# Four places in an attention and mixture-of-experts kernel where an instruction moves in its engine's order

## The chip, the cores and the metric

The kernel runs on one core of a Trainium2 chip. The metric is the device time of one launch in microseconds, less is better. The engines are named as in the profile: PE (TensorE, matrix products), PEld (its weight loads), DVE (VectorE), ACT (ScalarE), POOL (GpSimd), SP (SyncE, which issues most DMA transfers).

## What is computed

Causal attention with a bias from running sums, then a two-level mixture of experts over its output. All data are float32.

```python
cum = np.cumsum(np.maximum(s, 0.0), axis=-1)
bias = -(cum[:, :, :, None] - cum[:, :, None, :])
scores = np.where(causal, -1000000000.0, q @ k.T / 8 + np.minimum(bias, 0.0))
attn = softmax(scores)            # 8 batches, 8 heads, 576 tokens, 64 wide
x = (attn @ v) as rows of 512     # 4608 tokens
# each token: best of 4 groups, then best of its 4 experts; weight = both softmax values
out[tok] = weight * (relu(x[tok] @ w1[g, e]) @ w2[g, e])   # 512 -> 1024 -> 512
```

## The kernel before

**Attention.** The 64 heads go in 32 pairs, and the main loop takes one head a step. A step's instructions stand in an order written out by hand: strings of letters (`ORDERS`, `FIRST`, `OPENING`), one letter for one piece of work, so that PE, DVE, ACT and POOL each get theirs interleaved. For the step's own head there are the scores (B, five products into PSUM, then `exp` on ACT with b and the causal mask on POOL with e), for the head before it the product with v (C, evacuated on ACT with v), and for a head four steps on the row maximum of the scores (A0 to A5: products `pm`, which DVE reduces with a, tile `mx`, into `mc`). The six pieces of the row maximum are, in the order of their numbers, 288 keys (the first half of the last query tile), 64, 192, 320, 448, and 288 again (its second half). `pm` has two PSUM banks, so a product `pm` waits until DVE has reduced the one two before it.

When a pair is done its output is divided by the sums of the softmax. DVE transposes the sums in blocks (Y, L333), inverts one column (Z, L339), transposes back (W, `back`, L344) and multiplies (K, `finish`, L354, which writes `xT`). W stands in the even steps; K comes at the start of the odd step that follows, since that step asks for it (`need`).

**Running sums.** At the start DVE rounds s up to 0 and scales it (`r1`), makes running sums of 64 heads by 576 tokens in one instruction (`c2`, L440), splits them in a high and a low part (`cumh`, named `ch` in the profile, L441 and L442), and SP copies rows of them into the operand tiles `WA` of the first four pairs (`load_a`, L177). `ones(i)` sets the rows of ones in `WA[i]`: for 0 and 2 on DVE, for 1 and 3 on POOL. The first products of all (L208) need the high and low rows.

**Router.** Every four pairs one batch of 576 tokens is routed (`Router.batch`, called a piece at a time with R): logits, a transposition of the last 64 tokens into rows (`pr`, L754, copied to `xrt` on ACT, L756), choice of group and expert, places in the experts' lists (`rows`, `val`, and products `pi` for token numbers, `pw` for weights, L863). PSUM tiles of the scores, of the logits and of `pr` share a ring of three banks (`ring`, pool `ps_s`); the router also has one bank of its own (`kept`, pool `ps_t`).

**Experts.** The first expert begins while the last batch is still being routed. Its PE order is fixed by `behind` (the first named instruction comes after the second): `pi` of the last batch stands after 8 of the products `py` of its second layer (`made[8]` comes after it). From `pi` DVE makes the row numbers by which POOL gathers the tokens. What the first expert has beyond 256 tokens is done as a small extra tile (`Tile`, name "r"), whose scaled output `yo` goes into a tile of `rows(u)`: one buffer that the 256 tokens' output `yr` has just used. Output rows leave by indirect DMA from POOL (`scatter`, L967). The other 15 experts follow, with weights loaded a megabyte at a time (`raw`, L1001) and split in two parts on ACT, POOL and DVE.

Outside the order by hand (DVE, ACT and POOL from the last two steps of the attention to the second expert) a scheduler sets the order.

Of the kernel before, what the change touches and what calls it, by code (L numbers as in the profile page):

```python
# [8 lines left out]
F32 = mybir.dt.float32  # L9
# [4 lines left out]
ALU = mybir.AluOpType  # L14
# [5 lines left out]
B, H, S, D = 8, 8, 576, 64  # L20
P = 128
NTOK = B * S
DM = 512
# [14 lines left out]

KT = [(P * k, min(P, S - P * k), S - P * k) for k in range(5)]
Q2 = 256  # L40
W2 = S - Q2


# [68 lines left out]
def attention(tc, qk, v, s, wr, xs, st):  # L112
# [3 lines left out]
    with ExitStack() as ctx:  # L116
# [36 lines left out]
        def split(p, h, later=False):  # L153

            r, w, wb = raws[p], WA[p % NA], WB[p % NBB]
            nc.scalar.copy(w[0:64, :, h, QO:], r[:, h])

            def low(a):
                i = nc.gpsimd.tensor_tensor(  # L159
                    out=wb[64 * a:64 * a + 64, a, h], in0=r[:, h, a], in1=w[0:64, a, h, QO:].bitcast(F32),  # L160
                    op=ALU.subtract)
                if gate and gate[0] is not None:
                    tc.add_manual_dep(i.ins, gate[0].ins.name, mybir.DependencyInfo(
                        mybir.DependencyClass.Sync, mybir.DependencyReason.DATA), reason="behind the product")

            for a in (KA, QA):
                if later:
                    push("G", p, lambda a=a: low(a))
                else:
                    low(a)  # L170

        def load_a(p):
            w = WA[p % NA]
            if p < 4:
                for h in range(2):
                    n = 2 * p + h
                    nc.sync.dma_start(w[64:66, KA, h, QO:].bitcast(F32), cumh[n:n + 1].bitcast(F32))  # L177
            else:
                nc.sync.dma_start(w[64:66, KA, :, QO:].bitcast(F32), cumd[2 * p:2 * p + 2].rearrange("h a s -> a h s"))

# [251 lines left out]

        def ones(i):
            for a in (QA, KA):
                (nc.gpsimd if i % 2 else nc.vector).memset(WA[i][64:66 if a == QA else 68, a].bitcast(F32).rearrange("p h q -> p (h q)"), 1.0)

        ones(0)
        nc.vector.tensor_scalar(out=r1, in0=s0, scalar1=0.0, scalar2=8.0, op0=ALU.max, op1=ALU.mult)

        nc.vector.tensor_tensor_scan(out=c2, data0=r1, data1=r1, initial=0.0, op0=ALU.add, op1=ALU.max)  # L440
        nc.vector.tensor_copy(cumh[:, 0], c2)  # L441
        nc.vector.tensor_tensor(out=cumh[:, 1], in0=c2, in1=cumh[:, 0].bitcast(F32), op=ALU.subtract)  # L442
        ones(2)
        ones(1)

        mask = sm.tile([P, S], F32, name="mask", tag="mask", bufs=1)
# [12 lines left out]
        load_a(1)  # L459
        for h in range(2):  # L460
            split(0, h)
        load_b(0)
        for t in VT:
            nc.gpsimd.memset(t[:, 0:NB, 2], 1.0)
# [9 lines left out]
        def store_sums():  # L474
# [8 lines left out]

        ORDERS = [o.split() for i, o in enumerate((
# [4 lines left out]
        FIRST = [o.split() for i, o in enumerate((  # L489
# [122 lines left out]
class Router:  # L612
# [121 lines left out]
    def batch(self, b, x):  # L734
# [14 lines left out]
        self.logits(b, x)  # L749
        yield  # L750

        ps = self.ps_s(f"pr{b}")
        for c in range(4):
            nc.tensor.transpose(ps[:64, c * P:(c + 1) * P], x[:, c, 512:S], ident)  # L754
        xr = sm.tile([64, DM], F32, name=f"xrt{b}", tag="xrt", bufs=1)
# [181 lines left out]
def moe(tc, w1, w2, xs, st, out):  # L937
# [3 lines left out]
    with ExitStack() as ctx:  # L941
# [87 lines left out]
        def rows(u):  # L1029
            return sp.tile([P, 3, DM], F32, name=f"yr{u}", tag="yr", bufs=1)  # L1030
# [217 lines left out]
        class Tile:  # L1248
# [8 lines left out]
            def items(self):  # L1257
                u, w = self.u, self.w

                th, tl = xhl(u, 1)  # L1260
                h = self.xg[:, 0:2].rearrange("p a c -> p (a c)")
                pss = {}

                def split(hi, lo, src, j, cols):
                    ps = pt.tile([P, 512], F32, name=f"pr{u}_{j}", tag="pt")
                    for c in range(4):
                        nc.tensor.transpose(ps[:, c * P:(c + 1) * P], src[:, c * P:(c + 1) * P], ident)
                    pv = ps.rearrange("p (a c) -> p a c", c=cols)
                    return (nc.scalar.copy(hi, pv),
                            V.tensor_tensor(out=lo, in0=pv, in1=hi.bitcast(F32), op=ALU.subtract))  # L1270

                def x():
                    self.split = split(th[:, :, 0:P], tl[:, :, 0:P], self.xg[:, 2], "x", P)

                def hidden(i, c0):
                    if c0 == 0:
                        pss[i] = acc(f"pu{u}_{i}")
                    for c in range(c0, c0 + 2):
                        for n, (a, b) in enumerate(((th, w.h), (tl, w.h), (th, w.l))):
                            nc.tensor.matmul(pss[i], a[:, c, 0:P], b[i][:, c], start=(c == 0 and n == 0),  # L1280
                                             stop=(c == 3 and n == 2))
                    if c0 == 2:
                        nc.scalar.activation(h[:, i * 512:(i + 1) * 512], pss[i], AF.Relu)

                def turn(j):
                    cs = slice(2 * j, 2 * j + 2)
                    split(th[:, cs, P:], tl[:, cs, P:], h[:, j * 512:(j + 1) * 512], j, 256)

                def y(f0):
                    if f0 == 0:  # L1290
                        pss["y"] = acc(f"pv{u}")
                    for f in range(f0, f0 + 2):
                        fs = slice(P + P * (f % 2), 2 * P + P * (f % 2))
                        for n, (a, b) in enumerate(((th, w.h), (tl, w.h), (th, w.l))):
                            nc.tensor.matmul(pss["y"], a[:, f // 2, fs], b[2 + f // 4][:, f % 4],
                                             start=(f == 0 and n == 0), stop=(f == 7 and n == 2))
                    if f0 == 6:
                        yo = rows(u)[:, 0]
                        V.tensor_scalar(out=yo, in0=pss["y"], scalar1=self.cw, scalar2=None, op0=ALU.mult)
                        scatter(yo, self.ids)  # L1300

                return ([x] + [lambda i=i, c=c: hidden(i, c) for i in range(2) for c in (0, 2)] +
                        [lambda j=j: turn(j) for j in range(2)] + [lambda f=f: y(f) for f in (0, 2, 4, 6)])
# [69 lines left out]
        with tc.manual_schedule(engines={ENG.PE}):  # L1373
            run(X)
            behind(tc, first.turns[0], st.av[0])
            behind(tc, st.av[2], first.turns[3])
            for i in st.put_off:
                behind(tc, i, first.split[1])
            for i in range(4):
                behind(tc, wts[0].casts[i], first.highs[1 if i < 2 else 3])  # L1380
            behind(tc, first.highs[2], st.evacs[-1])
            behind(tc, wts[0].lows[14], rest.last)
            h = first.h_items()
            run(h)
            made = first.products
            behind(tc, made[34], st.logged)
            behind(tc, st.turning, made[54])
            behind(tc, made[55], st.turned)
            behind(tc, made[77], st.counted)
            behind(tc, st.powers, wts[0].casts[11])  # L1390
            for i in [st.thirds] + first.rounds[4:]:
                behind(tc, i, wts[0].casts[15])
            Y, R = first.y_items(), rest.items()
            del made[:]
            run(Y[:5])
            behind(tc, made[8], st.listed[0])
            behind(tc, st.listed[2], made[-4])
            run(Y[5:6])
            run(R[:1])
            with after(tc, rest.split[1]):  # L1400
                by_slot(idp, idlp, 0, E)
                listed = V.tensor_copy(ids, idp)
            part = [st.lists[:, j].rearrange("p e h -> p h e") for j in range(NV)]
            cwl = idl
            with after(tc, listed):
                V.tensor_copy(idlp, part[3])
                V.tensor_tensor(out=idlp, in0=idlp, in1=part[4], op=ALU.add)
                V.tensor_tensor(out=cwl, in0=idlp, in1=part[2], op=ALU.add)
                V.tensor_copy(idlp, cwl)
                by_slot(cws, idlp, 0, 1)  # L1410
            run(Y[6:] + R[1:5])
            W = wts[1].load((first.rounded, rest.split[0], None, None), (None, rest.split[1], None, None))
            run(W[:8])
            low = wts[1].low
            X, Z = slots[1].x_items(), first.z_items()
            run(X[:2] + R[5:6] + X[2:])
            with after(tc, *slots[1].split):
                run(W[8:12])
            run(R[6:7] + Z)
            with after(tc, *slots[1].split):  # L1420
                run(W[12:])
            run(R[7:])
            with after(tc, low):
                slots[2].gather()
# [244 lines left out]
```

## Time and profile before

| | |
|---|---|
| median of 3 runs | 899.67 us (899.33 to 900.61) |
| the profiled execution | 901.16 us, its span 899.4 us |
| busy in the span: PE, DVE, ACT, POOL | 95%, 77%, 68%, 69% |
| attention alone, about 30 to 420 us | PE busy 98 to 99% of each stretch |
| first expert's end, 440 to 460 us | PE busy 17.41 of 20 us, granted clock 0.91 |
| second expert's start, 480 to 500 us | PE busy 18.42 of 20 us |

PE is the engine that is nearly always busy; the others have room. Matmuls are pipelined and their modelled ends overlap, so a short wait of PE can show as a start that comes late without an idle time beside it: the distance of two starts tells more than the busy share.

### The profile page before, as it was taken

What the parts mean: (1) busy time and instruction counts of PE and PEld (TensorE: products, weight loads), DVE (VectorE), ACT (ScalarE), POOL (GpSimd) and SP (SyncE); (2) the same over time, 40 slices, a digit from 0 to 9 for tenths busy, and PEclk for the clock granted to TensorE, in tenths of its full rate; (3) what the DMA queues carried; (4) which work ended last, traced back from release to release, by engine and by line L of the source; (5) the groups of instructions that cost most, each with busy time, mean ns of one, the idle gap of its engine ahead of it and who ended that gap; (6) DMA issues with size and microseconds to landing.
All of it is one profiled execution on the core that took longest, in us unless ns stands there. A gap on an engine that the chain in (4) does not pass through costs nothing. (4 is left out here: it accounts for less than half of the span.)

```text
span 899.4 us, 17619 instructions
## 1 busy us (share of the span) xinstructions
PE 851.9 (95%) x5657; PEld 771.6 (86%) x5657; DVE 689.0 (77%) x1987; ACT 610.3 (68%) x1310; POOL 620.0 (69%) x733
## 2 busy tenths in 40 slices
PE   4899999999999999999999999999999999999993
PEld 3788788888888788887888999999999999999992
DVE  7677686858778686866874799889988888988830
ACT  3688787887878787867565566676676766676650
POOL 8898576766667576724877565776668778877750
PEclk9999999999999999999999999999999999999997
DMA  7766665556545665324656445555565555565410
GB/s 151 190 166 175 149 166 145 150 145 165 157 106 155 167 165 132 92 82 170 209 197 210 169 155 208 178 196 174 190 222 185 193 192 197 206 234 210 165 45 24
DMA packets 65004, 148.10 MB, mean 165 GB/s; under 512 B 7588, under 2 KB 40996, under 8 KB 54728
## 3 DMA queue, kind: packets, MB, share of 16 engines
q1 hardware_dynamic: 55020, 126.98, 47.3%
q0 software_dynamic: 7488, 18.89, 5.7%
q10 hardware_dynamic: 2396, 1.02, 0.4%
q8 instruction: 47, 0.77, 0.4%
q14 instruction: 53, 0.43, 0.2%
HBM read 108.97 MB, written 19.69 MB: 143 GB/s over the span
## 5 line engine op out<-in xcount | busy, mean ns | idle before, releaser
L1006 POOL TENSOR_TENSOR wl<-raw,wh 128x512 fp32r<-128x512 f32 x182 | 232.4, 1299 | 47.8 <-ACT wh L1003 34.7
L159 POOL TENSOR_TENSOR WB<-r,WA 64x576 fp32r<-64x576 f32 x128 | 181.6, 1419 | 32.4 <-DVE xT L354 17.3
L216 DVE CUSTOM_DVE_ANT_0 mx<-pm,mask 128x192 bf16<-128x192 f32 (+4 forms) x320 | 128.2, 418 | 35.7 <-PE pm L208 31.3
L1003 ACT CAST wh<-raw 128x512 fp32r<-128x512 f32 x256 | 154.0, 618 | 0.7 <-issue 0.4
L1123 PE MATMUL ph<-xh,wh 128*128 128x256 f32 (+13 forms) x512 | 141.5, 303 | 4.4 <-ACT xh L1079 2.0
L208 PE MATMUL pm<-WA 66*128 66x288 f32 (+4 forms) x384 | 123.9, 353 | 16.1 <-DMA WA<-ch 9.8
L1123 PE MATMUL ph<-xl,wh 128*128 128x256 f32 (+13 forms) x512 | 138.4, 302 | 0.3
L265 PE MATMUL ps<-WA 68*128 68x320 f32 (+4 forms) x384 | 132.8, 350 | 1.4 <-ACT pu L275 1.4
L284 POOL TENSOR_SCALAR_AFFINE_SELECT pt<-pt 128x128 f32<-128x128 f32 (+2 forms) x192 | 64.7, 341 | 87.0 <-ACT pt L275 82.6
L305 PE MATMUL po<-pt,VT 128*128 128x256 f32 (+3 forms) x512 | 118.1, 350 | 0.3 <-issue 0.3
L1193 PE MATMUL py<-hl,wh 128*128 128x256 f32 (+13 forms) x448 | 116.1, 306 | 2.1 <-DVE hl L1119 1.9
L1193 PE MATMUL py<-hh,wh 128*128 128x256 f32 (+13 forms) x448 | 114.2, 304 | 0.0
L267 PE MATMUL ps<-WB 128*128 128x320 f32 (+4 forms) x384 | 109.8, 299 | 0.0
L1239 DVE STREAM_TRANSPOSE yr<-yT 32x384 f32<-32x384 f32 (+1 forms) x208 | 104.4, 502 | 4.3
L305 PE MATMUL po<-pu,VT 128*128 128x320 f32 (+1 forms) x384 | 105.1, 381 | 0.0
L1075 DVE STREAM_TRANSPOSE xt<-xg 32x256 f32<-32x256 f32 (+1 forms) x208 | 102.5, 493 | 3.2
L1123 PEld LDWEIGHTS ph<-xh,wh 128*128 128x128 f32 x512 | 94.9, 189 | 8.0 <-ACT xh L1079 4.1
L208 PEld LDWEIGHTS pm<-WA 66*128 66x128 f32 (+1 forms) x384 | 68.1, 189 | 36.8 <-DVE mc L216 21.5
L305 PEld LDWEIGHTS po<-pt,VT 128*128 128x128 f32 x512 | 87.6, 191 | 12.6 <-issue 0.7
L1123 PEld LDWEIGHTS ph<-xl,wh 128*128 128x128 f32 x512 | 94.8, 189 | 1.8 <-DVE xl L1080 1.3
L1123 PE MATMUL ph<-xh,wl 128*128 128x256 f32 (+13 forms) x512 | 92.6, 299 | 0.0
L1117 ACT ACTIVATE hh<-ph 128x256 fp32r<-128x256 f32 (+13 forms) x128 | 53.9, 422 | 56.2 <-PE ph L1123 55.4
(245 smaller groups left out, 1809.8 us busy)
## 6 DMA issues: line engine op xcount, KB each, us to landing
raw<-in_w_dram SPq DMA_DIRECT2D x64, 1024.0 KB
WB<-WA SPq DMA_DIRECT2D x64, 288.0 KB
r<-in_qk_dram SPq DMA_DIRECT2D x31, 576.0 KB
VT<-in_v_dram SPq DMA_DIRECT2D x32, 384.0 KB
xs<-xr SPq DMA_DIRECT2D x15, 512.0 KB
xs<-xrt SPq DMA_DIRECT2D x7, 128.0 KB
xg<-xs,ids POOLq DMA_INDIRECT x46
out_dram<-yr,ids POOLq DMA_INDIRECT x43
```

The lines of the kernel that those rows point to most:

```text
L159: i = nc.gpsimd.tensor_tensor(out=wb[64 * a:64 * a + 64, a, h], in0=r[:, h, a], in1=w[0:64, a, h, QO:].bitcast(F32), op=ALU.subtract)
L208: nc.tensor.matmul(ps[:rows, :cw], WA[i][0:66, QA, h, QO + q0:QO + q0 + rows], WA[i][0:66, KA, h, QO + c0:QO + c0 + cw], start=True, stop= ...
L216: nc.vector.tensor_tensor_reduce(out=tmp[:rows, :cw], in0=ps[:rows, :cw], in1=mk[:rows], scale=1.0, scalar=-3.0e38 if c0 == 0 else mo, op0 ...
L265: nc.tensor.matmul(ps[:rows, o:o + w], WA[i][0:68, KA, h, QO + k0:QO + k0 + rows], WA[i][0:68, QA, h, QO + q0:QO + q0 + w], start=True, st ...
L267: nc.tensor.matmul(ps[:rows, o:o + w], WB[p % NBB][:, KA, h, k0:k0 + rows], WB[p % NBB][:, QA, h, q0:q0 + w], start=False, stop=True)
L305: i = nc.tensor.matmul(po[0][:, qa - base:qb - base], VT[p % NVT].rearrange("p t a d -> p (t a d)")[:, (3 * t + 1 + h) * 64:][:, 0:P], x[: ...
L1003: self.casts.append(nc.scalar.copy(h[:, j], raw[:, j]))
L1006: self.low = nc.gpsimd.tensor_tensor(out=l[:, j], in0=raw[:, j], in1=h[:, j].bitcast(F32), op=ALU.subtract)
L1075: V.transpose(dst[:, 0:n, :, j], src[:, 0:n, :, i])
L1123: self.products.append(nc.tensor.matmul(pss[f][:, :cap], w[f // 4][:, c, (f % 4) * P:(f % 4 + 1) * P], x[:, c, :cap], start=(c == 0 and w ...
L1193: self.products.append(nc.tensor.matmul(pss[c][:, :cap], w[2 + f // 4][:, f % 4, c * P:(c + 1) * P], x[:, f, :cap], start=(f == 0 and w is ...
L1239: V.transpose(dst[:, 0:n, :, i], src[:, 0:n, :, j])
```

## The change

Four edits. (1) In the even steps W goes from ahead of A4 to just ahead of the last A5, behind a further a. (2) `pr` of all batches but the last goes into the router's own bank. (3) The running sums are made, split and (for the first head) copied in two pieces, tokens 0 to 287 and 288 to 575, and `ones(2)` goes to POOL, behind the low parts of the first pair. (4) `pi` of the last batch comes after 24 products `py` instead of 8; and the extra tile's `yo` is put in `yT`, not in a tile of `rows(u)`.

```diff
+CUT = 288
 def load_a(p):
                 for h in range(2):
                     n = 2 * p + h
-                    nc.sync.dma_start(w[64:66, KA, h, QO:].bitcast(F32), cumh[n:n + 1].bitcast(F32))
+                    for a, e in ((0, CUT), (CUT, S)) if n == 0 else ((0, S),):
+                        nc.sync.dma_start(w[64:66, KA, h, QO + a:QO + e].bitcast(F32), cumh[n:n + 1, :, a:e].bitcast(F32))
...
-                (nc.gpsimd if i % 2 else nc.vector).memset(WA[i][64:66 if a == QA else 68, a]...
+                (nc.gpsimd if i else nc.vector).memset(WA[i][64:66 if a == QA else 68, a]...
...
-        nc.vector.tensor_tensor_scan(out=c2, data0=r1, data1=r1, initial=0.0, op0=ALU.add, op1=ALU.max)
-        nc.vector.tensor_copy(cumh[:, 0], c2)
-        nc.vector.tensor_tensor(out=cumh[:, 1], in0=c2, in1=cumh[:, 0].bitcast(F32), op=ALU.subtract)
-        ones(2)
+        for a, e in ((0, CUT), (CUT, S)):
+            x = slice(a, e)
+            nc.vector.tensor_tensor_scan(out=c2[:, x], data0=r1[:, x], data1=r1[:, x], initial=c2[:, a - 1:a] if a else 0.0,
+                                         op0=ALU.add, op1=ALU.max)
+            nc.vector.tensor_copy(cumh[:, 0, x], c2[:, x])
+            nc.vector.tensor_tensor(out=cumh[:, 1, x], in0=c2[:, x], in1=cumh[:, 0, x].bitcast(F32), op=ALU.subtract)
         ones(1)
...
         for h in range(2):
             split(0, h)
+        ones(2)
         load_b(0)
...
-            "W e A4 C5 e C6 b a A5",
+            "e A4 C5 e C6 b a W A5",
...
-        ps = self.ps_s(f"pr{b}")
+        ps = (self.ps_t if b < B - 1 else self.ps_s)(f"pr{b}")
...
-                        yo = rows(u)[:, 0]
+                        yo = yT.rearrange("p c t -> p (c t)")[:, 0:DM] if u == "r" else rows(u)[:, 0]
...
-            behind(tc, made[8], st.listed[0])
+            behind(tc, st.listed[0], made[23])
+            behind(tc, made[24], st.listed[0])
```

What this does to the engines' orders is shown at three places. DVE in an even step of the middle of the attention and at the start of the odd one after it, before (`pm_0` is the product with 64 keys, `pm_3` that with 448, each reduction is followed by a row that reads its result into `mc`):

```order
L216 ISA mx_1_0_2669,mc_157<-pm_1_0_2645,mask 128x192
L216 ISA mc_157 128x1
L344 STREAM_TRANSPOSE st_2563<-rc_2586 128x576
L216 ISA mx_0_0_2679,mc_157<-pm_0_0_2671,mask_151 64x64
L216 ISA mc_157 64x1
L354 TENSOR_TENSOR xT_2133<-vals_2328,st_2563 128x576
L216 ISA mx_3_0_2693,mc_157<-pm_3_0_2674,mask 128x448
```

and in the change:

```order
L218 ISA mx_1_0_2673,mc_158<-pm_1_0_2649,mask 128x192
L218 ISA mc_158 128x1
L218 ISA mx_0_0_2682,mc_158<-pm_0_0_2675,mask_152 64x64
L218 ISA mc_158 64x1
L346 STREAM_TRANSPOSE st_2567<-rc_2590 128x576
L356 TENSOR_TENSOR xT_2137<-vals_2332,st_2567 128x576
L218 ISA mx_3_0_2697,mc_158<-pm_3_0_2677,mask 128x448
```

The transposition W and the 64-key reduction have changed places, so W now stands directly ahead of the product that reads it; the 448-key reduction is still behind all three. This is so for 28 of the 32 pairs.

DVE at the start of the program in the change (`cl` holds s, `r1` and `c2`; before, L440, L441 and L442 each went over all 576 tokens, and two memsets of `WA` came before the first reduction):

```order
L440 TENSOR_SCALAR cl<-cl 64x576
L444 SCALAR_TENSOR_TENSOR cl<-cl 64x288
L446 CAST ch<-cl 64x288
L447 TENSOR_TENSOR ch<-cl,ch 64x288
L444 SCALAR_TENSOR_TENSOR cl<-cl 64x288
L446 CAST ch<-cl 64x288
L447 TENSOR_TENSOR ch<-cl,ch 64x288
L218 ISA mx_4_0_192,mc_157<-pm_4_0_188,mask 128x288
```

Six instructions of half the length stand where there were three, and the memsets are gone to POOL.

PE in the first expert's second layer, in the change (`hh`, `hl` are the two parts of the hidden values, `wh` the high part of the weights):

```order
L1198 MATMUL py_1_6517<-hh_6376,wh_2_6273 128x256
L1198 MATMUL py_1_6517<-hl_6377,wh_2_6273 128x256
L868 LDWEIGHTS rows_6156
L868 MATMUL pi_6163<-val_6158,rows_6156 128x128
...
L1198 MATMUL py_1_6517<-hh_6376,wh_3_6276 128x256
```

Before, `pi` stood in the middle of `py_0`; 16 products, the rest of `py_0` and half of `py_1`, have come ahead of it.

## Rows read from the trace of the kernel before

**Rows 1.** The list of waits of PE: releaser, total us, times, longest
```profile
PE ph L1123 <- DVE yrr L1299: 1.6, 1, 1.6
PE pmt L231 <- ACT xrt L756: 1.5, 6, 0.3
```
**Rows 2.** Timeline of the start: start, duration, engine, line, operation
```profile
4.74 1.35 DVE L440 TENSOR_TENSOR_SCAN cl<-cl 64x576 f32<-64x576 f32 x1
6.12 0.75 DVE L441 CAST ch<-cl 64x576 fp32r<-64x576 f32 x1
6.90 0.75 DVE L442 TENSOR_TENSOR ch<-cl,ch 64x576 fp32r<-64x576 f32 x1
7.68 2.60 SPq L177 DMA_DIRECT2D WA<-ch  x4
9.83 0.95 PE L208 MATMUL pm<-WA 66*128 66x288 f32 x3 [9.83 <-DMA WA<-ch]
...
11.10 1.25 PE L208 MATMUL pm<-WA 66*128 66x320 f32 x3 [0.31 <-DVE mc L216]
```
**Rows 3.** Timeline, a pair without router work on DVE, DVE and PE
```profile
186.37 0.76 DVE L344 STREAM_TRANSPOSE st<-rc 128x576 f32<-128x576 f32 x1
186.87 0.50 PE L208 MATMUL pm<-WA 66*64 66x64 f32 x2
187.13 0.22 DVE L216 CUSTOM_DVE_ANT_0 mx<-pm,mask 64x64 bf16<-64x64 f32 x1
187.47 0.76 DVE L354 TENSOR_TENSOR xT<-vals,st 128x576 f32<-128x576 f32 x1
188.15 0.62 DVE L216 CUSTOM_DVE_ANT_0 mx<-pm,mask 128x448 bf16<-128x448 f32 x1
189.27 0.36 PE L208 MATMUL pm<-WA 66*128 66x448 f32 x1
```
**Rows 4.** Timeline, a pair with router work on DVE
```profile
215.80 0.62 DVE L216 CUSTOM_DVE_ANT_0 mx<-pm,mask 128x448 bf16<-128x448 f32 x1
216.48 0.47 PE L208 MATMUL pm<-WA 66*128 66x448 f32 x1
```
**Rows 5.** Timeline, the 448-key products in pairs of two other kinds
```profile
54.57 0.47 PE L208 MATMUL pm<-WA 66*128 66x448 f32 x1 [0.15 <-DVE mc L216]
228.38 0.47 PE L208 MATMUL pm<-WA 66*128 66x448 f32 x1 [0.18 <-DVE mc L216]
```
**Rows 6.** Timeline behind `pr`: ACT's `exp`, and the product that waits for it
```profile
248.60 0.54 ACT L275 ACTIVATE pu<-ps 128x448 f32<-128x448 f32 x1
249.24 0.37 PE L265 MATMUL ps<-WA 68*128 68x320 f32 x1
```
**Rows 7.** Timeline around `pi`, and products at either clock
```profile
442.20 0.28 PE L1193 MATMUL py<-hh,wh 128*128 128x256 f32 x1
444.28 0.88 DVE L856 TENSOR_TENSOR val<-col,pk 128x320 bf16<-128x320 bf16 x2
445.22 0.45 PE L863 MATMUL pi<-val,rows 128*128 128x128 bf16 x5 [1.90 <-DVE val L856]
447.15 0.41 PE L1193 MATMUL py<-hh,wh 128*128 128x256 f32 x1
447.37 0.41 PE L1193 MATMUL py<-hl,wh 128*128 128x256 f32 x1
450.98 1.28 DVE L911 TENSOR_TENSOR val<-col,pk 128x320 bf16<-128x320 bf16 x3 [0.24 <-ACT pk L900]
453.76 2.08 PE L1193 MATMUL py<-hh,wl 128*128 128x256 f32 x16
```
**Rows 8.** Stages: start:end, us, busy of PE, PEld, DVE, ACT, POOL, clock
```profile
446.20:449.60 3.40, 3.40 (x18) 3.40 (x18) 2.92 (x15) 0.00 (x0) 1.65 (x2) 0.51 0.00 0
```
**Rows 9.** Timeline, the outputs of the first expert: POOL and DVE
```profile
482.06 1.00 POOL L967 DMA_INDIRECT out_dram<-yr,ids  x1 [0.30 <-issue]
489.77 0.75 DVE L1299 TENSOR_SCALAR yrr<-pvr,cws 128x512 f32<-128x512 f32 x1 [5.69 <-DMA out_dram<-yr,ids]
```

More of the change, by code (lines that the diff above doesn't have):

```diff
@@ L434, in ones @@
             for a in (QA, KA):
-                (nc.gpsimd if i % 2 else nc.vector).memset(WA[i][64:66 if a == QA else 68, a].bitcast(F32).rearrange("p h q -> p (h q)"), 1.0)
+                (nc.gpsimd if i else nc.vector).memset(WA[i][64:66 if a == QA else 68, a].bitcast(F32).rearrange("p h q -> p (h q)"), 1.0)
         ones(0)
         nc.vector.tensor_scalar(out=r1, in0=s0, scalar1=0.0, scalar2=8.0, op0=ALU.max, op1=ALU.mult)
-        nc.vector.tensor_tensor_scan(out=c2, data0=r1, data1=r1, initial=0.0, op0=ALU.add, op1=ALU.max)
-        nc.vector.tensor_copy(cumh[:, 0], c2)
-        nc.vector.tensor_tensor(out=cumh[:, 1], in0=c2, in1=cumh[:, 0].bitcast(F32), op=ALU.subtract)
-        ones(2)
+        for a, e in ((0, CUT), (CUT, S)):
[4 more added lines that the diff above has]
+            nc.vector.tensor_tensor(out=cumh[:, 1, x], in0=c2[:, x], in1=cumh[:, 0, x].bitcast(F32), op=ALU.subtract)
         ones(1)
```

## The prediction

> **What bounds the kernel.** The page's busy shares come first: PE works 95% of the span, no other engine over 77%. So an edit pays only where it takes a wait from PE or gives it one. The list of PE's waits says which waits these are: among them one of 1.6 us for `yrr` (the extra tile's `yo`) and six of 0.25 on the mean for the copies of `pr` [rows 1]. The timeline then gives each place: the start, where PE has nothing to do before 9.83 [rows 2]; the pairs in the loop [rows 3 to 5]; the turn behind `pr` [rows 6]; `pi` and the products around it [rows 7], with the granted clock from the table of stages [rows 8]; the scatter of the first expert [rows 9]. In the loop nearly all of PE's loss is in starts a few tenths late, so distances of starts count there, not idle times. All terms are made in the profiled execution, 901.16 us (span 899.4); it is 1.5 above the median of 899.67, so the sum is taken off the median.
>
> **Start: -0.8 (0 to -1.2).** Before, the scan begins at 4.74, the low part ends at 7.65, the copies are issued from 7.68 and the first product starts at 9.83, 2.15 later [rows 2]. A half as long instruction costs more than half: the reductions of 64 and of 448 columns take 0.22 and 0.62 [rows 3], that is 0.15 fixed and 0.1 per 100 columns. So I estimate the half scan at 0.75 and the half cast and subtraction at 0.45 each, 1.65 together and about 0.07 between them. The first piece is ready at 6.46 instead of 7.68, the second at 8.18, and by the same 2.15 they land at 8.6 and 10.3. The 320-key product, which stood at 11.10, needs the second piece and can start at 10.3: 0.8 earlier. The first piece alone would give 1.2. What follows at that distance is the end at nothing, if head 0's fourth issue or POOL's two memsets hold up the operands of the next heads as long as PE has gained; POOL's later high and low parts are the work that has to hide them.
>
> **W moved: +3.2 (0 to +4.5).** W itself stays; what matters is who stands behind it. Sorted by what else DVE has in the step, the 28 pairs are of these kinds.
> (a) 12 pairs have router work on DVE. Work is always ready there, so DVE is late with or without W in front of the 64-key reduction; the 448-key reduction has the same work ahead of it as before, and the 448-key product of the odd step, which needs its bank, starts 0.68 behind it [rows 4]. That distance is the bound and doesn't change: 0.
> (b) 9 pairs are like 186.37. There W filled a time in which DVE waited for the 64-key product of 186.87 anyway: the reduction begins at 187.13, when that product is done [rows 3]. Now DVE waits first and does W after: `xT` and the 448-key reduction come a W later, 0.70 (what the start of one instruction is from that of the next, 187.47 to 188.15). The 448-key product would be released at 188.15 + 0.68 = 188.83 and starts at 189.27, so 0.44 is spare; 0.26 is left. Over pairs I take 0.20 to 0.34, 0.25 in the middle: 9 x 0.25 = 2.25.
> (c) 6 pairs are like that of 228.38, where the product already waits 0.18 for DVE [rows 5]. DVE is late there too, but less: 0 to 0.13, I take 0.05: 0.3.
> (d) The pair of 54.57, whose product waits 0.15 already [rows 5], has no spare at all: 0.7.
> Together 3.2. The lower end is none of it, if PE makes a late 448-key product good before its step ends; the upper takes 0.34, 0.13 and 0.7: 9 x 0.34 + 6 x 0.13 + 0.7 = 4.5.
> The other side of the exchange, the 64-key bank free earlier by W in (a) and (c), gives PE nothing, since the next product to want that bank is followed by the 448-key one that is still bound.
>
> **`pr` in the router's bank: -0.3 (0 to -1.5).** PE's wait for `xrt`, 6 x 0.25 [rows 1], goes. But the next score product but one waits for a bank of the same ring: it starts at 249.24, 0.10 behind the `exp` that ends at 249.14 [rows 6], and ACT works without a gap up to there. So most of the wait turns up there: I take 0.05 each. The whole 1.5 is the far end.
>
> **`pi` later: -3.3 (-1.8 to -3.4).** Before, after eight products `py` (from 442.20, 0.12 apart) PE has nothing until `val` ends at 445.16: a wait of 1.90 [rows 7]. With 24 ahead PE is at 442.20 + 24 x 0.12 = 445.08 when it gets to `pi`: the wait is gone, -1.8. [...] `pi` itself and the gather behind it come at the same time as before, since `val` sets them. The later router products wait for `val` as before (the last of three from 450.98 is done near 452.3) and are taken in with as many `py` fewer to put in front of them; nothing says that there are too few.
> [...]
>
> **`yo` in `yT`: -1.6 (0 to -1.6).** `yo` waited 5.69 for the scatter that still read its buffer, issued at 482.06 and done by 489.7 [rows 9]; PE's products behind it waited 1.6 [rows 1]. The buffer of `yT` is free then. Next to want `yT` is ACT's first copy of the following expert, and it must now wait for the extra tile's scatter: issued near 484, and by the same 7.65 done near 491.7. PE reaches that copy's products, with the 1.6 won, only some microseconds later, so I take it as hidden; if not, the gain is gone.
>
> **Sum.** -0.8 + 3.2 - 0.3 - 3.3 - 1.6 = -2.8; 0.2 is given back by products that `pi` used to stand ahead of: -2.6. Median 899.67 - 2.6 = **897.1**.
>
> **Rivals.**
> *W costs nothing.* The delay in (b) to (d) is taken up: PE's order has other products ahead, and a late 448-key product pushes only its own chain of reductions. For it: in (b) 0.44 is spare, and the 0.26 over it is a difference of two small numbers. Against it: the waits of 0.15 and 0.18 show that this product is bound where DVE is late [rows 5]. Then -5.8: 893.9.
> *The clock spell stays.* It may not be owed to that one wait. For it: the spell begins at 446.20 [rows 8], 1 us after the wait has ended at 445.22 [rows 7]. Against it: of the waits of PE in these stretches that of 1.90 is the only long one, and the spell follows next to it. Then `pi` gives 1.8 and a little less: the sum is -1.1, 898.6. [...]
> *The other side: W is a wait in every pair.* `xT` now reads what the instruction just ahead of it wrote, and (a) and (c) may have as little to spare as (d). Each pair then costs up to 0.34, 28 x 0.34 = 9.5, against 3.2: +3.7, 903.4. It decides from 0.27 a pair: 28 x 0.27 = 7.6 is 1.8 above the 5.8 that the other edits give, and the kernel is slower by 0.2%. For it: the products of (c) and (d) that already wait. Against it: at the start, where a cast reads what the scan has just written, it begins 0.03 behind it (6.12 after 4.74 + 1.35) [rows 2].
> *The start's and the extra tile's gains are eaten*, by POOL's memsets or by the copy into `yT`: -0.2 to -1.8, 898.5 on the mean.
>
> **How the numbers follow.** Chances: the forecast 0.45, W free 0.23, clock stays 0.15, gains eaten 0.10, slower 0.07. A measurement here can tell 0.2%, 1.8 us: faster is below 897.9, slower above 901.5. Faster takes W free and, of the forecast with bounds that reach 1 us to either side, four fifths, and a little of the others: 0.23 + 0.36 + 0.03 = 0.62. Slower is the other side: 0.07. The rest, 0.31, is the same. The range is from W free with the full start and clock, 893.6, to the clock staying with W at its upper end, 898.6 + 1.0 = 899.6; the slower side beyond it and something below it are left out.
>
> **What would show it.** Right: the first `pm` at about 8.6 and the 320-key product near 10.3; no wait before `pi`, and granted clock 1.00 all through 445 to 456; no wait of `yo`, and ACT's first `yT` copy of the next expert not held by a DMA; `pmt` without a wait and the score product behind it hardly earlier; in pairs like 186.37 the 448-key product 0.2 to 0.3 later relative to the step's start, in pairs like 215.80 not. Wrong: the loop from 30 to 420 us as long as before (W free) or 6 or more longer (a wait in every pair); a spell at the lower clock near `pi`.

## The result

The changed kernel is slower: 906.77 us (median of 10 runs, 904.52 to 908.65) beside 901.85 for the kernel before (10 runs on the same chips, 899.33 to 904.80); the ratio is 1.006, interval 1.0047 to 1.0073. By the ratio that is 5.4 more (4.2 to 6.6), where 2.6 less was forecast. The profiled execution took 907.36, its span 905.6 beside 899.4.

Where it came from is read by setting the same product of PE against itself in the two traces. Between the rows below the difference hardly moves, or moves in steps that the text names.

| product of PE, start before | start after | later by |
|---|---|---|
| `ps`, 19.66 | 20.64 | 0.98 |
| `ps`, 48.29 | 49.28 | 0.99 |
| `ps`, 54.88 | 57.34 | 2.46 |
| `po`, 64.06 | 68.18 | 4.12 |
| `ps`, 199.87 | 207.12 | 7.25 |
| `po`, 419.87 | 430.78 | 10.91 |
| `py`, 451.96 | 459.47 | 7.51 |
| `ph`, 488.50 | 496.43 | 7.92 |
| `py`, 500.03 | 506.09 | 6.06 |
| `ph`, 870.01 | 876.11 | 6.10 |

So `pi` gave back 3.4 and `yo` 1.9, nearly as forecast; the start cost 1.0 in this execution, and the loop cost 9.9, nearly all in the 28 pairs in which W moved ("later by" is what PE has lost up to that product; where it falls, PE has won).

The list of waits of PE in the changed kernel (releaser, total us, times, longest):

```profile
PE pm L210 <- DVE mc L218: 13.4, 30, 1.6
PE pm L210 <- DMA WA<-ch: 11.2, 2, 9.9
...
PE ps L267 <- ACT pu L277: 2.4, 7, 1.1
```

The waits of `pi`, of `pmt` for `xrt` and of `ph` for `yrr` [rows 1, 7] are gone; seven score products wait for ACT now where one did (1.4 us), which is the wait of `pmt` come back (it starts 0.42 earlier in each batch and the score product behind it 0.38 later than that). `pm`'s waits for DVE have grown from 3.2 us in 16 waits to 13.4 in 30: W.

The pair that answers to [rows 3], timeline of DVE and PE after:

```profile
193.83 0.22 DVE L218 CUSTOM_DVE_ANT_0 mx<-pm,mask 64x64 bf16<-64x64 f32 x1 [0.71 <-PE pm L210]
194.17 0.78 DVE L346 STREAM_TRANSPOSE st<-rc 128x576 f32<-128x576 f32 x1
194.99 0.83 DVE L356 TENSOR_TENSOR xT<-vals,st 128x576 f32<-128x576 f32 x1
195.74 0.61 DVE L218 CUSTOM_DVE_ANT_0 mx<-pm,mask 128x448 bf16<-128x448 f32 x1
196.42 0.47 PE L210 MATMUL pm<-WA 66*128 66x448 f32 x1 [0.28 <-DVE mc L218]
196.73 0.28 PE L267 MATMUL ps<-WA 68*128 68x256 f32 x1
```

The 448-key reduction starts 1.91 behind the 64-key one, where it was 1.02, so it is 0.89 late and not 0.70; of that 0.44 is spare. And PE loses some 0.1 more in starting again: its next product is 0.31 behind the 448-key one, where it was 0.21 without a wait (189.27, 189.48). The nine pairs of this kind lost 0.47 to 0.57 each, 4.6 together. Three rows of the kernel before, for this and for what follows:

```profile
189.48 0.28 PE L265 MATMUL ps<-WA 68*128 68x256 f32 x1
...
214.13 0.76 DVE L344 STREAM_TRANSPOSE st<-rc 128x576 f32<-128x576 f32 x1
214.82 0.17 DVE L216 CUSTOM_DVE_ANT_0 mx<-pm,mask 64x64 bf16<-64x64 f32 x1
```

Why 0.89? W lasts 0.76 to 0.78 either way. Ahead of an instruction that doesn't read its result it counts for 0.70, because the next one starts before it ends: W at 214.13 and the 64-key reduction at 214.82 in the kernel before. Ahead of `xT`, which reads it, it counts for 0.81 (194.17 to 194.99 here, and in 27 of the 28 pairs; in the other one something stands between), and `xT` is 0.07 longer here. The same 0.11 and the order around it show in a pair with router work, which answers to [rows 4]:

```profile
221.51 0.20 DVE L218 CUSTOM_DVE_ANT_0 mx<-pm,mask 64x64 bf16<-64x64 f32 x1
221.85 0.78 DVE L346 STREAM_TRANSPOSE st<-rc 128x576 f32<-128x576 f32 x1
...
222.66 0.76 DVE L356 TENSOR_TENSOR xT<-vals,st 128x576 f32<-128x576 f32 x1
223.33 0.62 DVE L218 CUSTOM_DVE_ANT_0 mx<-pm,mask 128x448 bf16<-128x448 f32 x1
...
224.01 0.47 PE L210 MATMUL pm<-WA 66*128 66x448 f32 x1 [0.58 <-DVE mc L218]
```

From the first of the three (here the 64-key reduction, there W) to the 448-key reduction it is 1.82 here and was 1.67. The twelve pairs with router work lost mostly 0.15 each and at most some 0.3, 2.1 in all. Of the six with a long `xT` five lost nothing, since `xT` fell otherwise against POOL's work (0.95, 1.25 before); one lost 0.3 (`xT` 1.13).

The dearest pair is that near 54 us [rows 5]: two rows of the timeline before, the timeline after, and the stage behind it in the changed kernel (start:end, us, busy of PE, PEld, DVE, ACT, POOL, granted clock, DMA):

```profile
53.23 0.75 DVE L354 TENSOR_TENSOR xT<-vals,st 128x576 f32<-128x576 f32 x1
53.35 1.90 POOL L159 TENSOR_TENSOR WB<-r,WA 64x576 fp32r<-64x576 f32 x1
```

```profile
54.37 1.45 POOL L160 TENSOR_TENSOR WB<-r,WA 64x576 fp32r<-64x576 f32 x1
54.46 1.98 DVE L356 TENSOR_TENSOR xT<-vals,st 128x576 f32<-128x576 f32 x1
...
57.03 0.47 PE L210 MATMUL pm<-WA 66*128 66x448 f32 x1 [1.64 <-DVE mc L218]
```

```profile
58.70:62.10 3.40, 3.40 (x14) 3.01 (x13) 1.83 (x6) 2.07 (x5) 1.89 (x3) 0.50 0.55 115
```

`xT`, made late by W, begins 0.09 behind a low part that POOL makes (`WB`) and ends 1.98 later; before, `xT` began first, took 0.75 and POOL's instruction took 1.90. PE waits 1.64 for it and then has a spell at the lower clock (granted 0.50; 1.00 in the stages on either side, 30 to 58.6 and 62.1 to 420 us): 1.5 and 1.6 are lost. The stages of `pi` show the granted clock 1.00 all through (440 to 460 us), as forecast.

The start, answering to [rows 2]:

```profile
6.55 6.28 SPq L179 DMA_DIRECT2D WA<-ch  x5
7.16 2.86 POOL L160 TENSOR_TENSOR WB<-r,WA 64x576 fp32r<-64x576 f32 x2 [0.93 <-ACT WA L157]
7.29 1.43 DVE L446 CAST ch<-cl 64x288 fp32r<-64x288 f32 x1
8.76 1.58 DVE L447 TENSOR_TENSOR ch<-cl,ch 64x288 fp32r<-64x288 f32 x1
9.90 0.95 PE L210 MATMUL pm<-WA 66*128 66x288 f32 x3 [9.90 <-DMA WA<-ch]
12.11 1.22 PE L210 MATMUL pm<-WA 66*128 66x320 f32 x3 [1.26 <-DMA WA<-ch]
```

Two things went otherwise. The first piece's copy is issued 1.1 earlier, and the first product starts no earlier. And the second cast and subtraction, 0.45 each by the forecast, took 1.43 and 1.58 beside POOL's low parts, so the second piece was ready at 10.34 and not at 8.2.

### The profile page after: what moved, and what is told of

It reads as the page before. It is cut to its first block, busy times and chain, and to the rows that moved or that the text cites. A ratio compares the mean times of both kernels' runs of the same rounds, so it can differ in the third digit from the quotient of the medians.

```text
span 905.6 us, 17623 instructions
## 1 busy us (share of the span) xinstructions
PE 850.7 (94%) x5657; PEld 771.2 (85%) x5657; DVE 694.5 (77%) x1988; ACT 611.4 (68%) x1310; POOL 617.7 (68%) x735
## 3 DMA queue, kind: packets, MB, share of 16 engines
q10 hardware_dynamic: 2396, 1.02, 0.4%
## 5 line engine op out<-in xcount | busy, mean ns | idle before, releaser
L210 PE MATMUL pm<-WA 66*128 66x288 f32 (+4 forms) x384 | 126.8, 360 | 26.6 <-DVE mc L218 13.4
L286 POOL TENSOR_SCALAR_AFFINE_SELECT pt<-pt 128x128 f32<-128x128 f32 (+2 forms) x192 | 62.0, 326 | 97.9 <-ACT pt L277 94.1
L277 ACT ACTIVATE pt<-ps 128x256 f32<-128x256 f32 (+2 forms) x192 | 76.5, 399 | 35.3 <-PE pm L210 14.0
```

What stands on the lines that cost most here:

```text
L210: nc.tensor.matmul(ps[:rows, :cw], WA[i][0:66, QA, h, QO + q0:QO + q0 + rows], WA[i][0:66, KA, h, QO + c0:QO + c0 + cw], start=True, stop= ...
```

## The experiments

All times are medians (5 to 12 runs a kernel), and ratios are to the kernel before on the same chip (900.48 to 900.86, 17 or 18 runs each). The runs were on several chips, so two of them are compared by their ratios.

**W alone.** The string of the even steps, nothing else.
```diff
-            "W e A4 C5 e C6 b a A5",
+            "e A4 C5 e C6 b a W A5",
```


> Only W is moved, all else as before. Theory A (read by setting PE's starts of the two traces side by side): the move costs 0.5 in each of 9 pairs without router work, about 0.17 in each of 12 with it, 0.2 over the six with xT beside POOL, and 1.5 in the pair near 54 us plus a spell at half clock behind it of 1.6: +9.8 in all. In every pair xT starts 0.81 behind W, where the 64-key reduction started 0.70 behind it. Rival B: the pair near 54 us and its spell are owed to the start, which is 1.0 late in the changed kernel: then W alone costs +6.7 and no spell is seen before 420 us. Rival C (the forecast): +3.2.

908.41, ratio 1.0081 (1.0066 to 1.0096), 7.3 more than before (5.9 to 8.7). In its trace PE is 0.05 late at 48 us, 3.16 at 64, 9.36 at 420: 9.3 of the loop's 9.9 are W's, and so is the spell at half clock (57.8 to 61.2 us); the start has no part in them. That is theory A's sum for the loop, and the spell, which rival B left out, speaks against B, though the time alone is nearer to B's 6.7. The pair near 54 us is as in the changed kernel (`xT` 1.98 beside POOL's 1.46). Of the waits:
```profile
PE pm L208 <- DVE mc L216: 13.5, 33, 1.6
...
PE pi L863 <- DVE val L856: 1.9, 1, 1.9
```
The whole program is only 6.1 longer in this trace than in that of before. `pi` waits its 1.9 here as there, but no spell at half clock follows (1.5), and `yo` meets no late scatter (1.75), though neither was edited. So the spell behind `pi` and the wait of `yo` are no fixed losses, and W alone was spared both.

**The same, with the one pair put back.** The changed kernel, with W at its old place in the step of the pair near 54 us.
```diff
+            if step == 4:
+                order = [[o for o in order[0] if o != "W"], order[1]]
+                order[0].insert(order[0].index("e", order[0].index("A1", 20)), "W")
```


> The changed kernel, but in one pair, that near 54 us, W stands where it stood before. Theory A (that pair alone costs 1.5, and the spell at half clock behind it 1.6): no spell before 420 us and 3.1 less than the changed kernel. Rival (the spell comes whatever happens there, or xT is held by POOL without W too): 0 to 0.7 less, and a spell before 70 us.

904.54, ratio 1.0045 (1.0032 to 1.0058). `xT` takes 0.74 again, and there is no spell:
```profile
53.05 0.74 DVE L356 TENSOR_TENSOR xT<-vals,st 128x576 f32<-128x576 f32 x1
53.18 1.89 POOL L160 TENSOR_TENSOR WB<-r,WA 64x576 fp32r<-64x576 f32 x1
54.40 0.47 PE L210 MATMUL pm<-WA 66*128 66x448 f32 x1 [0.20 <-DVE mc L218]
```
In the trace theory A holds: PE is 6.4 late at 420 us, where it was 10.9 in the changed kernel; 3.1 of the difference lies between 54 and 64 us, nearly all the rest is a start that came 1.2 earlier. In the medians the gain is smaller than the 3.1 expected: the ratio falls from 1.0060 to 1.0045, some 1.4. Not every run of the changed kernel has the spell (four of its ten show a mean granted clock of 0.993 or more, and take 904.5 to 905.5), and the two intervals leave room for the rest.

**W followed by something that doesn't read it.** W moved as in the first run, and `xT` behind the 448-key reduction (`vals` and `sums` of a pair are taken at their first write, so that K may stand there).
```diff
-            "C0 B2 A4 B0 A2 S v e O H C1 ...
+            "C0 B2 A4 K B0 A2 S v e O H C1 ...
```


> W moved and nothing else of the change; and xT stands behind the 448-key reduction, so that W is followed by an instruction that doesn't read it. Theory A (what costs is that W and xT together, xT waiting for all of W, stand ahead of the 448-key reduction): this reduction starts 1.0 behind the 64-key one, as it did before in the pairs without router work (1.02), where it was 1.83 with W alone moved; the 448-key product is not late, and the kernel is within -1 to +1.5 of before. Rival (a late xT costs as much through px): +3 to +8.

903.11, ratio 1.0024 (1.0010 to 1.0038): by the ratios 5.1 less than W alone and 2.2 more than before (0.9 to 3.4), between what theory A and the rival expected. In the pair of [rows 3]:
```profile
190.17 0.22 DVE L216 CUSTOM_DVE_ANT_0 mx<-pm,mask 64x64 bf16<-64x64 f32 x1 [0.69 <-PE pm L208]
190.51 0.78 DVE L345 STREAM_TRANSPOSE st<-rc 128x576 f32<-128x576 f32 x1
...
191.21 0.59 DVE L216 CUSTOM_DVE_ANT_0 mx<-pm,mask 128x448 bf16<-128x448 f32 x1
191.73 0.76 DVE L355 TENSOR_TENSOR xT<-vals,st 128x576 f32<-128x576 f32 x1
192.31 0.36 PE L208 MATMUL pm<-WA 66*128 66x448 f32 x1
192.40 0.52 DVE L216 CUSTOM_DVE_ANT_0 mx<-pm,mask,mc 128x288 bf16<-128x288 f32 x1
...
192.98 0.36 PE L208 MATMUL pm<-WA 66*128 66x192 f32 x1
```
W counts for 0.70 again (190.51 to 191.21), the 448-key reduction is 1.04 behind the 64-key one, and its product isn't late. The loss has gone on to the next reader: the 288-key reduction is behind `xT` now, and the 192-key product that needs its bank starts 0.58 behind that reduction and about 0.2 late, `px` 0.1 more. So the nine pairs of this kind lose 0.3 each and no longer 0.5; the twelve with router work, which lost 0.15 with W alone, now lose nothing. In the nine W at its old place ran while DVE waited for a product; at the new one its 0.7 is on DVE's path, whichever product shows it.

**`xT` later with W in place**, beside **`pr`, `pi` and `yo` alone**. The second has these three edits of the change and no other; the first adds the K of the diff above.

> Only pr, pi and yo are changed; W and the start are as before. Theory A: pr -0.25, pi -3.4 with 0.4 given back near 460 us, yo -1.85: -5.1, with no spell at half clock between 440 and 460 us. Rival (the clock spell is not owed to the wait ahead of pi): -3.5 and a spell near 446 us.

> As the run with only pr, pi and yo changed, and besides it xT stands behind the 448-key reduction, not ahead of it (vals and sums of a pair are taken later, at their first write; DVE's order differs in nothing else, the other engines' orders in nothing). Theory A (the 448-key reduction is what PE's 448-key product waits for in 18 pairs, and 0.18 of wait with 0.11 of restart hang on it): -2 to -5 against the run without it. Rival: PE's wait moves to the 288-key product ahead or to px, which needs xT 0.6 later: 0 to +2.

`pr`, `pi`, `yo`: 897.48, ratio 0.9961 (0.9947 to 0.9976): 3.5 less (2.2 to 4.8), and 4.2 between the profiled executions (against its lateness at 440 us PE is 2.3 earlier at the first `py` behind the wait and 3.4 at 449.5, since no spell comes; it gives back 0.7 by 460 us at `prr_x` and `pur`, and wins 1.74 at `yo`). Theory A's 5.1 is too much; the rival has the number and not the reason, since there is no spell near 446 us. With `xT` later: 897.38, 0.9956 (0.9942 to 0.9970): no difference that can be told. The 448-key product came 0.2 to 0.35 earlier in 18 pairs. In the twelve with router work the 192-key product and `px` behind it gave all of it back, as the rival says; the six with a long `xT` kept 0.1 to 0.3 each, and the pair near 54 us alone lost 0.85.

**The start alone**, and **all but W**.

> Only the start is changed (running sums in two pieces, ones(2) on POOL), all else as before. Theory A: +1.0, all of it by 13 us, because the second cast and subtraction take 1.4 to 1.6 instead of 0.45 beside POOL's low parts, and the first product still starts at 9.8 to 9.9 though its copy is issued 1.1 earlier. Rival B: +4, with a stall and a half clock near 54 us. Rival C (the forecast): -0.8.

> The changed kernel with W where it stood before, and nothing else taken back. Theory A: what W costs is the whole of the loss: 896.5 to 898.5, 8 to 10 less than the changed kernel, within 1 of the run with pr, pi and yo alone; the second cast or subtraction takes 1.4 or more beside POOL's low parts. Rival (the start is a loss of its own): +1 to +2 against the run with pr, pi and yo alone.

The start alone: 900.19, ratio 0.9991 (0.9978 to 1.0004): from 2.0 less to 0.4 more, so a loss of 1.0 is excluded and the forecast's 0.8 less is not. All but W: 896.87, 0.9959 (0.9944 to 0.9975), within 1 of the run without the start. Theory A was right for W and wrong to give the start a loss of 1.0 as a rule. From here to the changed kernel, 0.9959 to 1.0060, W costs some 9.1. Alone it costs 7.3; the intervals of the two overlap, but a difference of this sign is to be expected, since in its trace W alone was spared the spell and the wait that the other edits take away here. In the trace of the start alone:
```profile
6.90 0.30 DVE L446 CAST ch<-cl 64x288 fp32r<-64x288 f32 x1
7.04 3.00 POOL L160 TENSOR_TENSOR WB<-r,WA 64x576 fp32r<-64x576 f32 x2
7.23 1.54 DVE L447 TENSOR_TENSOR ch<-cl,ch 64x288 fp32r<-64x288 f32 x1
9.42 0.95 PE L210 MATMUL pm<-WA 66*128 66x288 f32 x3 [9.42 <-DMA WA<-ch]
10.68 1.25 PE L210 MATMUL pm<-WA 66*128 66x320 f32 x3 [0.31 <-DVE mc L218]
```
Here the cast started 0.14 ahead of POOL and took 0.30; only the subtraction was held. Counted from the start of the scan the 320-key product comes after 6.4 (4.30 to 10.68), as before (4.74 to 11.10), and after 7.4 in the changed kernel's profile (4.66 to 12.11). Here it waits 0.31 for a reduction on DVE and not for the second piece: while the first product was late, an earlier second piece gained nothing.

**POOL kept from DVE's way**, in two ways, on top of `pr`, `pi`, `yo` and the start. First `ones(2)` ahead of the low parts:
```diff
+        ones(2)
         for h in range(2):
             split(0, h)
-        ones(2)
```


> pr, pi, yo and the start as in the change, W as before; but POOL sets the ones of the third pair ahead of the first pair's low parts and not behind them. Theory A (DVE's second cast and subtraction are held up because POOL's low parts run beside them; who starts first decides): both take 0.3 to 0.5, the second piece's copy is issued near 8.2 and the 320-key product starts by 10.7, 0.4 earlier than before and 1.4 earlier than in the change; the first product stays at 9.4 to 9.9, since its copy lands behind a load of 0.6 MB. Against the run with pr, pi and yo alone: -0.3 to -0.6. Rival (POOL's memsets hold DVE as its low parts do): cast and subtraction 1.4 to 1.6 and 0 to +1.0.

898.40, ratio 0.9973 (0.9961 to 0.9984), some 1.1 more than `pr`, `pi` and `yo` alone: the rival. The memsets held the cast as low parts do:
```profile
6.25 2.26 POOL L437 MEMSET WA<- 2x1280 f32 x2
7.29 1.38 DVE L446 CAST ch<-cl 64x288 fp32r<-64x288 f32 x1
8.60 2.98 POOL L160 TENSOR_TENSOR WB<-r,WA 64x576 fp32r<-64x576 f32 x2
8.71 1.59 DVE L447 TENSOR_TENSOR ch<-cl,ch 64x288 fp32r<-64x288 f32 x1
```
Then `ones(2)` back, and a wait of POOL's low parts for DVE's last subtraction (`halves`):
```diff
+        gate.append(halves)
         for h in range(2):
             split(0, h)
+        gate.clear()
```


> pr, pi, yo and the start as in the change, W as before; and POOL's low parts of the first pair wait until DVE has finished the second piece. Theory A (DVE was held by POOL's work beside it): the second cast takes 0.3 and the subtraction 0.45, the second piece is ready by 8.1, the 320-key product starts by 10.8; -0.5 to -1.0 against the same kernel without that wait, -0.3 to -0.7 against the run with pr, pi and yo alone. Rival (POOL's lows, now about 1 later, are missed by the first scores): 0 to +1.

896.82, 0.9965 (0.9951 to 0.9978). That POOL's low parts held DVE is shown: nothing is held, and the second piece is ready at 7.70.
```profile
6.89 0.33 DVE L446 CAST ch<-cl 64x288 fp32r<-64x288 f32 x1
7.25 0.45 DVE L447 TENSOR_TENSOR ch<-cl,ch 64x288 fp32r<-64x288 f32 x1
7.84 5.81 POOL L160 TENSOR_TENSOR WB<-r,WA 64x576 fp32r<-64x576 f32 x4 [0.79 <-issue]
9.60 0.95 PE L210 MATMUL pm<-WA 66*128 66x288 f32 x3 [9.60 <-DMA WA<-ch]
```
The gain that theory A expected of it (0.3 to 1.0) did not come: the time is that of `pr`, `pi` and `yo` alone all the same, since the first product still starts at 9.60, 3.45 behind the issue of its copy at 6.15.

**The load in front of the copy.** Three runs put the load of the second pair's q and k (0.6 MB) elsewhere: on ACT's queue from the start (on top of the ones first), on ACT's queue behind its first rounding (on top of the waiting low parts), and on SP behind the first pair's copies (the same).
```diff
-        load_raw(1)
...
+        load_raw(1, queue=nc.scalar)
```


> As the run with the ones first, and the load of the second pair's q and k is issued on ACT's queue and not on SP's. Theory A (the first piece's copy waits behind that load in its own queue): the first product starts 1.2 or more earlier than 9.4, near 8.0, and the 320-key product is then bound by the second piece near 9.9 to 10.3; 0.3 to 0.8 less than with the ones first. Rival (the load has the DMA engines, whatever queue it is in): the first product stays at 9.4 to 9.9.

> As the run in which POOL's low parts wait, and the load of the second pair's q and k is issued by ACT behind its first rounding, near 7.2, and not by SP at 2.7. Theory A (the first piece's copy lands late because that load is ahead of it): the copy, issued near 6.5, lands near 8.0, the first product starts 1.2 to 1.6 earlier, the 320-key product near 10.0: -0.6 to -1.1 against the run without that. Rival (the second pair's work, with its load 4 later, is then what PE waits for): 0 to +2.

> As the run in which POOL's low parts wait, and the load of the second pair's q and k is issued by SP behind the copies for the first pair, near 9.0, and not at 2.7. Theory A (a copy lands no sooner than a load that is in flight when it is issued, on whatever queue that load is): the first copy lands near 8.0, the first product starts 1.2 or more earlier than 9.6, the 320-key product near 9.5 to 10.0 where it was at 10.9; -0.8 to -1.3 against the run without that. Rival (a copy within the chip's memory takes 3 us whatever else runs): no change at the first product. Rival (the second pair is now late): the lead is gone again by 30 us, 0 to +2.

897.00, 0.9968 (0.9956 to 0.9979); 898.79, 0.9976 (0.9966 to 0.9986); 899.70, 0.9992 (0.9980 to 1.0005). The first product starts at 10.43, 11.16 and 8.35. On ACT's queue from the start, the load also delayed that of the first pair, so this run tells little (ACT's first rounding starts at 8.72, and at 5.52 with the ones first). In the second ACT issued the load at 5.72, ahead of the copy and not behind it as expected, and the copy, issued at 6.15 on another queue, landed when the load did (ACT starts to read the load at 11.11, the first product starts at 11.16). So the first product was 1.6 later, not 1.2 to 1.6 earlier:
```profile
5.72 0.57 ACTq L152 DMA_DIRECT2D r<-in_qk_dram  x1
6.15 4.24 SPq L179 DMA_DIRECT2D WA<-ch  x5
11.11 2.21 ACT L157 CAST WA<-r 64x1152 fp32r<-64x1152 f32 x2 [3.18 <-DMA r<-in_qk_dram]
```
In the third no load was in flight:
```profile
6.45 2.75 SPq L179 DMA_DIRECT2D WA<-ch  x3
8.35 0.95 PE L210 MATMUL pm<-WA 66*128 66x288 f32 x3 [8.35 <-DMA WA<-ch]
9.24 0.52 SPq L152 DMA_DIRECT2D r<-in_qk_dram  x1
```
Theory A holds for the copy: 1.9 from issue to product, and with a load in flight the first product came when ACT began to read that load, with the load on the copy's own queue (9.60 and 9.51, POOL's wait) as with it on the other (11.16 and 11.11). It fails for the time, which is 2.4 more than with POOL's wait alone where 0.8 to 1.3 less was expected: the other rival holds. ACT waits 6.64 for the late load, up to 14.69, and only then issues the copy of `tl` (the low part of the row maxima); the first score product waits 3.9 for it, until 20.42. The lead is gone by 20 us.

Of all these five are the fastest and not to be told apart: POOL's wait, all but W, the load on ACT's queue from the start, `xT` later, and `pr`, `pi` and `yo` alone, 896.8 to 897.5, 0.3 to 0.4% less than before. So what beats both kernels is the change without W; the start may be left out as well.

## Why the prediction was wrong

**W, +3.2 forecast, 9.3 measured in the loop** (W alone; 6.1 of it, in that trace, at the end of the program; 9.1 in time when all the other edits are in). This is the step that failed. The mechanism was seen: a later 448-key reduction, the bank, the product. Its size was not. (1) In kind (b) the W that comes behind the 64-key reduction was put at "0.70 (what the start of one instruction is from that of the next)". That is the distance to an instruction that doesn't read the result; to `xT` it is 0.81, and `xT` was a little longer in some pairs. (2) PE's new start, 0.1 after each wait, was left out. Together 0.5 and not 0.25 in nine pairs. (3) Kind (a) was put at 0 because "the 448-key reduction has the same work ahead of it as before". The work was the same, its order was not: 0.15 in most of twelve pairs, 2.1 together. (4) Kind (d), 0.7 forecast, met POOL's low part and cost 1.5 and a spell of 1.6. The upper end of 4.5 covers none of this, since it was built from the same 0.70 and the same 0.

**The rival of the other side** named one cause, "`xT` now reads what the instruction just ahead of it wrote", with 0.27 a pair as the point from which it decides; 9.3 over 28 pairs are 0.33. That this comes so near to its 0.34 is luck: 3.1 of it is one pair and its spell, which it didn't foresee, and the other 27 have 0.23 on the mean, from nothing to 0.55. It was turned down by a row misread: a cast that starts 0.03 behind the scan that it reads was taken for no cost. The row beside it in [rows 3] had the other half: `xT` at 187.47 is 0.76 long and the next starts at 188.15, 0.08 before its end. The cost is the difference of the two, 0.11.

**The start, -0.8.** Nothing was gained that can be told from noise, and two assumptions fell. "By the same 2.15" was the landing of a load in flight (ACT begins to read it at 9.71, the first product starts at 9.83), not the copy's own time (1.9 with no load in flight). And POOL was looked at for what the memsets delay on it, not for what it does to DVE beside it.

**`pr`, -0.3:** right, 0.04 to 0.05 a batch, for the reason given.

**`pi`, -3.3:** right in the profiled execution, wait and spell. The 1.5 that it has beside the 1.8 of the wait is read from the trace of before: the granted clock is 0.51 from 446.20 to 449.60 [rows 8], and 16 products there stand 0.22 apart (447.15 to 447.37) and not 0.12 as at a granted clock of 1.00 [rows 7]. In the changed kernel the clock is 1.00 there, and 3.4 came back. But the spell is not owed to the wait alone: W alone kept the wait of 1.9 and had no spell behind it, and in the run with the load behind the copies the granted clock fell to half at 37.14 us though PE had waited only 0.17 and 0.25 since the clock rose at 33.73. Of the 14 traces the five with such a spell have a mean granted clock of 0.992 or lower, the nine without 0.993 or more (all 14 are at the lower clock for their last 12 to 15 us, and no mean tells where a spell lies). By this sign 33 of 69 runs of the kernel before have one, and 15 of 64 of the eight kernels that have `pi` later and W in place. So the rival about the clock was partly right, and by an estimate from these counts the term is worth some 2.2 on the mean: 1.8 for the wait, and the 1.5 of a spell in a quarter of the runs (33 of 69 less 15 of 64). That, and the 0.7 given back where 0.2 was forecast, takes the -5.0 of `pr`, `pi` and `yo` together to -3.4; -3.5 was measured.

**`yo`, -1.6:** right (1.74 at the next `ph`, and 0.1 behind it); ACT's copy into `yT` was not held. The wait that it takes away is not a fixed one either: 1.6 before, 0.9 with the start alone, none with W alone.

Three side sums of the prediction are off by up to 0.3: the mean of the last rival is 898.7 and not 898.5, and the range would run from 893.4 to 899.9 by its own terms. Nothing hangs on them.

## What to carry to other kernels

An instruction that filled a wait of its engine was free there and cost elsewhere (W, 0.76 to 0.78 long, cost 0.5 in such pairs, and 0.15 where the engine had no wait to fill), so look at what the engine waits for behind it before moving it, and count it by the distance to its reader (0.81 here), not to its neighbour (0.70). Price an order by what each product's bank still needs, and add PE's new start to every wait (0.1 here). A copy of 2.2 KB was as late as the load of 0.6 MB in flight when it was issued, so cutting the work ahead of the copy gained nothing (issued 1.1 earlier, first product at 9.90 and not 9.83); and moving the load only pays if its own reader can wait, which it could not here (ACT waited 6.64, the first score product 3.9).

## What the hardware showed that was not expected

DVE and POOL held each other up in these traces, and the one that started a tenth later took longer: the same cast took 0.30 when it started 0.14 ahead of POOL's low part (the start alone) and 1.43 when it started 0.13 behind (the changed kernel); `xT` took 0.74 with POOL's low part at 1.89 when it started 0.13 ahead, or 1.98 with it at 1.45 when it started 0.09 behind. The held instruction shows no wait, only a longer time. Memsets of POOL went either way: the cast took 1.38 beside them with the ones first, and in the run with the load on ACT's queue from the start the subtraction, which took 1.53 to 1.59 beside low parts, took 0.45 beside one. What makes this difference was not shown.

A copy of 2.2 KB, 1.9 from issue to product with no load in flight, took 3.0 to 5.0 when it was issued early behind a load of 0.6 MB, on the load's own queue or another; issued late in the load's flight (7.68 in the kernel before) a copy of 4.5 KB took 2.15. ACT begins to read that load near the time of the first product: 9.71 and 9.83 before, 9.51 and 9.60 with POOL's wait, 11.11 and 11.16 with the load issued by ACT.
